# Linear attention into two mixture layers: the first batch's q loaded by tokens and turned on TensorE, its product in fp32, and two late weights in place of four

## The chip, the cores and the metric

The kernel runs on one core of a Trainium2 chip. The metric is the device time of one launch in microseconds (us), the median of three runs, lower is better. A core has five instruction queues that run beside each other: TensorE (PE in the rows, with PEld for its weight loads), VectorE (DVE), ScalarE (ACT), GpSimd (POOL) and SyncE (SP), which here issues nearly all DMA transfers. Each queue is worked off strictly in order, so an instruction that waits holds up all that stands behind it on its engine.

## The reference

q, k, v have shape (8 batches, 8 heads, 576 tokens, 64); all data are fp32.

```python
kv = np.einsum('bhsd,bhse->bhde', k, v)
out = np.einsum('bhsd,bhde->bhse', q, kv)
rms = np.sqrt(np.mean(out * out, axis=-1, keepdims=True) + 1e-06)
x = out / rms * g_norm                      # then 4608 tokens x 512
h = np.maximum(x @ w_in1, 0.0)              # 512 x 2048
x = (s * (h * h) + b) @ w_out1              # 2048 x 512
h = x @ w_in2
out = (h / (1.0 + np.exp(-h))) @ w_out2
```

## The kernel before, in words

The 4608 tokens are cut into nine blocks of 512 (`T`). Blocks 0 to 7 are the first 512 tokens of each batch; the ninth holds the 64 tokens (`REM`) that each batch has left over. Attention goes by pairs of heads, four pairs (`p`) in a batch, in `attention_pair`; `z` marks batch 0. A pair forms k'v on TensorE (`kv`, tile `kv_ps`), copies it out (`kv_out`, tile `kvf`, for batch 0 lent from a weight tile as `lent_wi10`), multiplies q by it (`o`, tile `o_ps`), does the same for the left-over tokens (`rem`, tile `r_ps`), and `normalize` squares (`sq`), sums (`part`, `ms` with tile `m_ps`), takes the root (`rms`), inverts (`inv`), spreads and scales to x. `split_x` then splits x into a rounded part `xh` and a rest `xl`.

A product of near-fp32 quality is made of three fast products on such halves (`mm3`: lines 208, 209, 210). So q of every pair is turned by VectorE (line 517, after four loads in which each run is 32 floats long), rounded on ScalarE (`q_hi`) and its rest taken on VectorE; k'v is split likewise (`kv_hi` and the `kvl` rest).

The first layer does blocks 0 to 4 directly. One unit (`unit`) is one of 16 slices of the hidden width: four products with `wi<m>` make tile `h` (12 matmuls), ScalarE and VectorE turn it into `gh`, four products with `wo<m>` add to the output sums `acc` (12 matmuls). The other blocks and the second layer use a scheme with seven products per four (lines 933 and 1074 to 1076). Before a weight can be used its 8-byte form must be loaded into `raw` and decoded by `decode`: ScalarE `mag`, VectorE `sign` and `top`, ScalarE `carry`, GpSimd `total`, ScalarE `hi`, VectorE `lo` (lines 309, 313, 318, 326, 332, 214, 220). Block 0 thus runs while the 32 weights of layer 1 are being decoded, in the order wi0, wi1, wo0, wi2, wo1 and so on.

Of these 32 the last `LATE` in that order are decoded otherwise: their room is taken from the decode buffers, so they are loaded, each in two halves (128x256), only after all the others are done and `turn` has closed the pool. With `LATE = 4` these are wo13, wi15, wo14 and wo15.

What order each queue gets is decided in Python at build time by `Plan.run`: it replays all steps with costs written beside them (`add(engines, key, ...)`) and issues, engine by engine, the step that it believes can start next, the smaller key first. While the replay's clock is under 40 it fills TensorE with small products on zeros (`warm_up`, line 1267, tile `warm`). These costs set the order alone; on the chip the queues wait for real events. Tiles in PSUM come from few banks: four under `acc`, two under `h`, two under `at`.

Of the kernel before, what the change touches and what calls it, by code (L numbers as in the profile page):

```python
# [133 lines left out]
def kernel(  # L134
# [36 lines left out]
    LATE = 4  # L171
# [111 lines left out]
    def decode(layer, kind, m, c, width, sfx, key, needs=(), quarter=None, made=()):  # L283
# [60 lines left out]
        add({"SP": 0.48}, key - 5 - 0.8 * (layer == 0 and (kind, m) == ("i", 1)), load, needs=needs, makes=[f(0)], takes=[raw], move=width * P * 8 / 3.6e5)  # L344
        key -= 0.5
# [101 lines left out]
    def attention_pair(bb, p, key, before=None):  # L447
# [11 lines left out]
        b["psk"], b["pso"], b["psr"] = ("at", ("k", me)), (acc, ("o", me)), ("at", ("r", me))  # L459

# [82 lines left out]
        for i in range(P // Q):  # L543
# [9 lines left out]
        add({ACT: 0.2}, key + 0.4, kv_hi, needs=[f("kvf")], makes=[f("kvh")], takes=[b["kvs"]], gives=[b["kvf"]])  # L553
        add({DVE: Port(0.2)}, key + 0.5, lambda e: rest(e, st["kvl"], st["kvf"], st["kvh"]), needs=[f("kvh")], makes=[f("kvl")],
            gives=[b["kvf"]])
        add(dve(S), key, q_turn, needs=[("q", bb, p, i) for i in range(P // Q)], makes=[f("qT")], takes=[b["qT"]],
            gives=[b["q"]])
        add(act(T), key + 0.4, q_hi, needs=[f("qT")], makes=[f("qh")], takes=[b["qs"]], gives=[b["qT"]])
        add(both(T), key + 0.5, lambda e: rest(e, st["ql"], st["qT"][:, :T], st["qh"]), needs=[f("qh")], makes=[f("ql")],
            gives=[b["qT"]])  # L560
        add({"PE": 0.682}, key + 1.5, o, needs=[f("kvl"), f("ql"), f("kvh"), f("qh")] + prev,
            makes=[f("o")], takes=[b["pso"]], gives=[b["kvs"], b["qs"]])
        add({"PE": 0.2}, key + 2.2, rem, needs=[f("kvf"), f("qT")], makes=[f("r")], takes=[b["psr"]],
# [5 lines left out]
        normalize(bb, p, key + 2, [f("o")], [b["pso"]], lambda: st["pso"])  # L569

    def normalize(t, p, key, needs, gives, src):
# [7 lines left out]
        def sq(e):  # L579
            st["sq"] = ap.tile([P, T], F32, tag="sq", name="sq")  # L580
# [28 lines left out]
        def x(e):  # L609
# [6 lines left out]
        add(act(T), key, sq, needs=needs, makes=[f("sq")], takes=[("sq", me)])  # L616
# [5 lines left out]
        add(dve(T), key + 0.8, x, needs=[f("spread")] + ([("x32", t, p - 1)] if p else []), makes=[("x32", t, p)],  # L622
            takes=[("x32", t)] if t < TP and p == 0 else [], gives=[("sq", me)] * (t < TP) + gives)
# [82 lines left out]
    def unit(u):  # L706
# [51 lines left out]
        add({ACT: 0.62} if layer == 0 else act(T), u + 0.3, g_hi, needs=[src], makes=[("gh", u)], takes=[gs])  # L758
# [384 lines left out]
    with tc.manual_schedule():  # L1143
# [10 lines left out]
        rem_t = ap.tile([P, 2, 2 * D], F32, name="rem_t")  # L1154
        lent["rem"] = lend("wo12")
        for t in (lent["rem"], rem_t):
            nc.gpsimd.memset(t[REM:], 0.0)
# [3 lines left out]
        for t in kvf_t:  # L1161
            nc.gpsimd.memset(t, 0.0)
# [161 lines left out]
```

## Time and profile before

| | before |
|---|---|
| median of three runs | 1564.57 us (1561.56 to 1564.99) |
| the profiled execution's own time | 1562.31 us |
| its span, first to last instruction | 1560.5 us |
| TensorE busy | 1539.7 us, 99% |
| VectorE busy | 1084.5 us, 69% |
| ScalarE busy | 854.7 us, 55% |
| GpSimd busy | 635.1 us, 41% |

A busy TensorE is not TensorE at work that counts: the products on zeros are busy time too, and an instruction's time in a row holds some 0.2 us of pipeline that overlaps the next one. The profiled execution is 2.26 us shorter than the median; 1.81 us of its time lie outside the span.

### The profile page before, as it was taken

The page shows a single profiled execution, that of the slowest core. Times are in us where ns is not written, and L with a number is a line of the kernel's source. Part 1 is how long each engine was busy: PE and PEld are TensorE (multiplying, and loading weights), DVE is VectorE, ACT ScalarE, POOL GpSimd, SP SyncE. Part 2 cuts the span into 40 slices and gives each one's busy share as a digit, 9 for nine tenths or more (in the row PEclk, how much of TensorE's full clock was granted, in tenths as well). Part 3 has the DMA queues.
Part 4 walks back from the last instruction along what each step waited for, and adds up shares of the span by engine and source line. Part 5 has one row for each costly group of instructions (what it writes and reads, how often), then busy time and mean ns, then how long its engine had stood idle before and what let it go on. Part 6 is the DMA issues. An engine that isn't in the chain of part 4 may idle for free.

```text
span 1560.5 us, 23102 instructions
## 1 busy us (share of the span) xinstructions
PE 1539.7 (99%) x7394; PEld 1259.0 (81%) x7394; DVE 1084.5 (69%) x1925; ACT 854.7 (55%) x1693; POOL 635.1 (41%) x584
## 2 busy tenths in 40 slices
PE   8998999999999999999999999999999999999998
PEld 6776878888888878888888788888888888888887
DVE  6887678878777577888888766775676566666521
ACT  5886566557666576667666544544454444444222
POOL 2331122111125234587548832772376246622410
PEclk9999999999999999999999999999999999999999
DMA  8855689988557878898988876878687766876684
GB/s 217 214 163 133 212 252 286 272 251 242 187 183 222 282 233 270 274 291 264 326 271 295 276 266 192 257 194 243 193 261 189 255 190 216 195 248 201 199 196 149
DMA packets 351514, 361.24 MB, mean 231 GB/s; under 512 B 175392, under 2 KB 236832, under 8 KB 351392
## 3 DMA queue, kind: packets, MB, share of 16 engines
q1 hardware_dynamic: 351264, 359.76, 76.4%
q8 instruction: 59, 0.97, 0.3%
q14 instruction: 63, 0.52, 0.1%
q0 software_dynamic: 128, 0.00, 0.0%
HBM read 272.63 MB, written 87.03 MB: 230 GB/s over the span
## 4 chain that ended last, share of the span: by engine, by line
PE 89%; DMA 4%; SPq 2%; DVE 2%; ACT 1%; issue 1%; POOL 0%; DVEq 0%; ACTq 0%
PE hp L933 28%; PE acc L1074 9%; PE acc L1075 9%; PE acc L1076 9%; PE h L208 5%; PE h L209 5%; PE h L210 5%; PE acc L208 4%; PE acc L209 4%; PE acc L210 4%; SPq L236 2%; DMA raw<-in_moe_w_out_dram 1%; PE kv_ps L503 1%; PE acc L773 1%; PE acc L772 1%; PE acc L774 1%
## 5 line engine op out<-in xcount | busy, mean ns | idle before, releaser
L933 PE MATMUL hp<-xo,win 128*128 128x512 f32 x2016 | 509.2, 390 | 1.1 <-DVE g L220 0.9
L933 PEld LDWEIGHTS hp<-xo,win 128*128 128x128 f32 x2016 | 377.1, 188 | 82.9 <-DVE tmp L958 4.1
L220 POOL TENSOR_TENSOR g<-tmp,g 128x512 fp32r<-128x512 f32 x192 | 249.3, 1307 | 306.2 <-ACT g L214 276.2
L1074 PE MATMUL acc<-g,wout 128*128 128x512 f32 x672 | 261.8, 390 | 0.8 <-DVE ya L1085 0.5
L1076 PE MATMUL acc<-g,wout 128*128 128x512 f32 x672 | 261.6, 389 | 0.0
L1075 PE MATMUL acc<-g,wout 128*128 128x512 f32 x672 | 261.5, 389 | 0.0
L1083 DVE TENSOR_TENSOR ya<-acc,ya 128x512 f32<-128x512 f32 x168 | 115.7, 689 | 128.3 <-PE acc L1076 120.6
L1074 PEld LDWEIGHTS acc<-g,wout 128*128 128x128 f32 x672 | 126.1, 188 | 28.0 <-DVE ya L1085 0.9
L1076 PEld LDWEIGHTS acc<-g,wout 128*128 128x128 f32 x672 | 126.1, 188 | 26.5
L1075 PEld LDWEIGHTS acc<-g,wout 128*128 128x128 f32 x672 | 126.2, 188 | 26.1
L214 ACT ACTIVATE g<-tmp 128x512 fp32r<-128x512 f32 x192 | 119.3, 629 | 24.4 <-PE acc L1076 10.3
L208 PE MATMUL acc<-gh,wo 128*128 128x512 f32 x320 | 131.2, 410 | 1.3 <-ACT wo L214 1.3
L739 ACT ACTIVATE h<-h 128x512 f32<-128x512 f32 x96 | 55.9, 582 | 139.0 <-PE h L210 137.0
L332 POOL TENSOR_TENSOR rq<-raw 128x256 uint32<-128x256 uint32 x72 | 47.2, 655 | 197.6 <-DVE raw L318 149.4
L208 PE MATMUL h<-xh,wi 128*128 128x512 f32 x320 | 126.9, 397 | 0.0
L1110 POOL TENSOR_TENSOR ya<-ya 128x512 f32<-128x512 f32 x84 | 108.1, 1316 | 45.7 <-DVE ya L1083 35.7
L209 PE MATMUL acc<-gh,wo 128*128 128x512 f32 x320 | 125.6, 392 | 0.6 <-DVE gh L222 0.4
L210 PE MATMUL acc<-gh,wo 128*128 128x512 f32 x320 | 125.4, 392 | 0.3 <-DVE wo L220 0.2
L209 PE MATMUL h<-xl,wi 128*128 128x512 f32 x320 | 125.4, 392 | 0.0
L210 PE MATMUL h<-xh,wi 128*128 128x512 f32 x320 | 125.2, 391 | 0.0
L958 DVE TENSOR_TENSOR tmp<-hp,tmp 128x512 f32<-128x512 f32 x144 | 98.9, 687 | 23.8 <-PE hp L933 19.5
L993 ACT ACTIVATE hp<-hp 128x512 f32<-128x512 f32 x96 | 55.6, 582 | 95.6 <-DVE hp L973 95.3
(164 smaller groups left out, 2685.1 us busy)
## 6 DMA issues: line engine op xcount, KB each, us to landing
wout<-wo SPq DMA_DIRECT2D x368, 256.0 KB, 4.1
win<-wi SPq DMA_DIRECT2D x144, 512.0 KB, 5.0
wi<-rq SPq DMA_DIRECT2D x96, 256.0 KB, 3.1
wo<-rq SPq DMA_DIRECT2D x96, 256.0 KB, 3.5
win<-wi SPq DMA_DIRECT2D x80, 256.0 KB, 4.1
raw<-in_moe_w_out_dram SPq DMA_DIRECT2D x38, 256.0 KB, 4.1
raw<-in_moe_w_in_dram SPq DMA_DIRECT2D x34, 256.0 KB, 4.2
q<-in_q_dram SPq DMA_DIRECT2D x112, 72.0 KB, 3.0
```

Of the source, the lines that this page charges most:

```text
L208: nc.tensor.matmul(ps, wh, xh, start=first, stop=False)
L209: nc.tensor.matmul(ps, wh, xl, start=False, stop=False)
L210: nc.tensor.matmul(ps, wl, xh, start=False, stop=last)
L214: nc.scalar.activation(hi, src, AF.Copy)
L220: eng[e].tensor_tensor(lo, src, f32(hi), op=ALU.subtract)
L933: nc.tensor.matmul(to, w[:, wn, f_], x_[:, xn], start=first and n == 0, stop=kk == KH - 1 and n == 2, skip_group_check=True)
L958: nc.vector.tensor_tensor(t, bank[me, a], tmp[b_, me], op=ALU.add)
L1074: nc.tensor.matmul(to, w[:, 0, dd], gh, start=a == 0, stop=False)
L1075: nc.tensor.matmul(to, w[:, 0, dd], gl, start=False, stop=False)
L1076: nc.tensor.matmul(to, w[:, 1, dd], gh, start=False, stop=a == 1)
L1083: nc.vector.tensor_tensor(y2[tp, i, d], st["ps"], y2[tp, i, d], op=ALU.add)
L1110: eng[e].tensor_tensor(y2[tp, i, d], y2[tp, i, d], y2[tp, j, d], op=ALU.add)
```

## The change

Four parts, all of the start of the kernel but the last. One: for batch 0, q is loaded as k and v are, with tokens on the 128 partitions, in one transfer a pair (`load_q0`), with one more for the left-over tokens of all heads (`load_q0_rem`); TensorE turns it by eight products with the identity (`q0_turn`, tile `q_ps`), ScalarE copies it out into token order (`q0_out`), and the product with k'v is one fp32 product (`o`) on `kvf` itself, without the halves. The left-over tokens are turned by TensorE later (`q0_rem_turn`, behind unit 1's products). Two: the squares of batch 0 go into the lent q tile in place of the one tile `sq`, and x gives that tile free. Three: the small loads of s, b and g_norm go to the front of GpSimd's queue, and the work on them becomes steps of the plan (`signs`, `norm_weights`, `offsets`). Four: `LATE = 2`, so wo13 and wi15 are decoded with the rest and only wo14 and wo15 are late. Some keys move with it.

```diff
-    LATE = 4
+    LATE = 2
...
+        def load_q0(e):
+            st["q"] = lend_flat(wtag["q"], 2 * T // P * D)
+            dma(
+                st["q"].rearrange("p (h c d) -> p h c d", h=2, d=D), q[bb, hh, :T, :].rearrange("h (p c) d -> p h c d", p=P)
+            )
+
+        def load_q0_rem(e):
+            lent["qrem"] = lend_flat("wo13", H * D)[:REM]
+            dma(lent["qrem"].rearrange("p (h d) -> p h d", d=D), q[bb, :, T:, :].rearrange("h p d -> p h d"))
+
+        def q0_turn(e):
+            lent["z", p] = lend_flat(wtag["qT"], 2 * DM)
+            st["psq"] = psum(b["psq"], "q_ps")
+            t = st["q"].rearrange("p (h c d) -> p h c d", h=2, d=D)
+            for c in range(NCH):
+                for j in range(2):
+                    nc.tensor.matmul(st["psq"][j * D:(j + 1) * D, c * P:(c + 1) * P], t[:, j, c, :], ident, start=True, stop=True)
+
+        def q0_rem_turn(e):
+            st["psr"] = psum(b["psr"], "r_ps")
+            nc.tensor.transpose(st["psr"][:, :REM], lent["qrem"][:, p * P:(p + 1) * P], ident[:REM, :REM])
+
+        def q0_rem_out(e):
+            st["qT"] = lent["z", p][:, T:T + REM]
+            copy(e, st["qT"], st["psr"][:, :REM])
...
+        def q0_out(e):
+            copy(e, lent["z", p][:, :T].rearrange("p (t c) -> p t c", t=P), st["psq"].rearrange("p (c t) -> p t c", t=P))
...
+            if z:
+                nc.tensor.matmul(st["pso"], st["kvf"], lent["z", p][:, :T], start=True, stop=True)
+            else:
+                mm3(st["pso"], st["kvh"], st["kvl"], st["qh"], st["ql"], True, True)
...
+        if z:
+            add({"SP": 0.48}, lk, load_q0, makes=[f("q")], takes=[b["q"]], move=0.73)
+            if p == 0:
+                add({"SP": 0.63}, lk + 5.9, load_q0_rem, makes=[("qr0",)], takes=[("wo13", 0)], move=0.4)
+        for i in range(0 if z else P // Q):
...
+        if z:
+            add({"PE": 0.5}, key + 0.2, q0_turn, needs=[f("q")], makes=[f("qt")], takes=[b["psq"], b["qT"]], gives=[b["q"]])
+            add({ACT: 0.56}, key + 0.25, q0_out, needs=[f("qt")], makes=[f("q32")], gives=[b["psq"]])
+            add({"PE": 0.95}, key + 1.5, o, needs=[f("kvf"), f("q32")], makes=[f("o")], takes=[b["pso"]])
+            add({"PE": 0.2}, key + 2.1, q0_rem_turn, needs=[("qr0",), f("kvf"), ("mm1o", 1, KD - 1)], makes=[f("qrt")], takes=[b["psr"]], gives=[("wo13", 0)])
+            add({ACT: 0.15, DVE: 0.15}, key + 2.15, q0_rem_out, needs=[f("qrt")], makes=[f("qT")])
...
-            st["sq"] = ap.tile([P, T], F32, tag="sq", name="sq")
+            st["sq"] = lent["z", p][:, :T] if z else ap.tile([P, T], F32, tag="sq", name="sq")
...
-        nc.scalar.activation(gn, eps, AF.Sqrt)
+        nc.scalar.activation(guess, eps, AF.Sqrt)
+        lent["rem"] = lend("wo12")
+        nc.vector.memset(lent["rem"][REM:], 0.0)
+        nc.gpsimd.dma_start(out=s_t, in_=s.rearrange("(o n) -> o n", o=1).to_broadcast([P, 1]))
+        nc.gpsimd.dma_start(out=b_t, in_=b.rearrange("(o n) -> o n", o=1).to_broadcast([P, 1]))
+        for j in range(2):
+            nc.gpsimd.dma_start(out=g0[j * D:(j + 1) * D, :], in_=g_norm.rearrange("(d o) -> d o", o=1))
...
+        add({DVE: 0.45}, -8, signs, needs=[("q32", 0, 0)], makes=[("signs",)])
+        add({ACT: 0.2}, -8, lambda e: nc.scalar.activation(root, mag_s, AF.Sqrt), needs=[("signs",)], makes=[("root",)])
+        add({DVE: 0.65}, -8, norm_weights, needs=[("root",)], makes=[("gn",)])
+        add({DVE: 0.3}, -1, offsets, needs=[("signs",), ("x32", 0, 1)], makes=[("b1",)])
...
-            split_x(0, p, -5 + 2 * p)
-        seq = [(t, p, KF * (t - 1) + (0.5 + (3.2 if t < LB else 1.6) * p if t > 1 else 0.75 + 3.4 * p)) for t in range(1, TP) for p in range(NP)]
+            split_x(0, p, -5.5 + 1.5 * p)
+        seq = [(t, p, KF * (t - 1) + (0.5 + (3.2 if t < LB else 2.0) * p if t > 1 else 0.75 + 3.4 * p)) for t in range(1, TP) for p in range(NP)]
...
-        last_block(KF * (TP - 2) + 9.5)
+        last_block(KF * (TP - 2) + 9)
```

The lists below give the instructions of one queue as they stand in the program; the number behind a name is that of its buffer.

SyncE's queue at the start of the program, before (`lent_wo<n>` are weight tiles that hold k, v and q of batch 0 meanwhile, `orem_d` is where left-over results go):

```order
L236 DMA lent_wo8_154<-in_k_dram 128x2x256
L236 DMA lent_wo8_154<-in_v_dram 128x2x256
L236 DMA lent_wo12_124<-in_k_dram 64x8x64
L236 DMA lent_wo12_124<-in_v_dram 64x8x64
L236 DMA lent_wo4_166<-in_q_dram 32x18x32 x4
...
L236 DMA lent_wo11_267<-in_v_dram 128x2x256
L236 DMA lent_wo7_292<-in_q_dram 32x18x32 x4
L236 DMA orem_d_76<-orem_241 128x64
L236 DMA raw_334<-in_moe_w_in_dram 128x4x256
L236 DMA raw_338<-in_moe_w_in_dram 128x4x256
```

and now, from the first q on:

```order
L236 DMA lent_wo4_155<-in_q_dram 128x2x256
L236 DMA lent_wo9_159<-in_k_dram 128x2x256
L236 DMA lent_wo9_159<-in_v_dram 128x2x256
L236 DMA lent_wo5_166<-in_q_dram 128x2x256
...
L236 DMA lent_wo13_193<-in_q_dram 64x8x64
L236 DMA lent_wo11_205<-in_k_dram 128x2x256
L236 DMA lent_wo11_205<-in_v_dram 128x2x256
L236 DMA lent_wo7_217<-in_q_dram 128x2x256
L236 DMA raw_235<-in_moe_w_in_dram 128x4x256
L236 DMA raw_240<-in_moe_w_in_dram 128x4x256
```

The sixteen q loads have become four, the store to `orem_d` no longer stands ahead of the first two weights (`raw`), and one load of left-over q is new.

ScalarE's queue around the decoding of the first weight wi0, before (`raw_334` is wi0, `raw_338` wi1):

```order
L581 ACTIVATE sq_358<-o_ps_326 128x512
L214 ACTIVATE xh_367<-x32_343 128x512
L231 COPY orem_387<-r_ps_290 128x64
L597 ACTIVATE rms_399<-m_ps_394,vecs_114 128x16
L214 ACTIVATE qTh_403<-lent_wi14_390 128x512
L309 ACTIVATE dw_422<-raw_334 128x512
L326 ACTIVATE raw_334<-raw_334 128x512
L231 COPY lent_wi10_129<-kv_ps_409 64x64 x2
L214 ACTIVATE kvh_444<-lent_wi10_129 128x128
L309 ACTIVATE dw_449<-raw_338 128x512
L581 ACTIVATE sq_458<-o_ps_376 128x512
```

and now, from the same step (`raw_235` is wi0, `raw_240` wi1, `lent_wi14` the turned q of head pair 3):

```order
L309 ACTIVATE dw_353<-raw_235 128x512
L231 COPY lent_wi14_338<-q_ps_339 128x512
L644 ACTIVATE rms_368<-m_ps_355,vecs_114 128x16
L326 ACTIVATE raw_235<-raw_235 128x512
L309 ACTIVATE dw_376<-raw_240 128x512
L326 ACTIVATE raw_240<-raw_240 128x512
L214 ACTIVATE xh_388<-x32_325 128x512
L628 ACTIVATE lent_wi14_338<-o_ps_372 128x512
L214 ACTIVATE xh_423<-x32_325 128x512
L214 ACTIVATE wi0_433<-dw_353 128x512
```

The roundings of k'v and q are gone; the copy of the turned q of pair 3 stands behind the first step on wi0, and the squares of pair 3 behind four steps on weights and one rounding of x.

TensorE's queue at the end of block 0, before (products with wi14, wo13 and wi15, between them attention of later batches):

```order
L208 MATMUL h_1549<-xh_630,wi14_1514 128x512
L208 MATMUL o_ps_1580<-qTh_1460,kvh_1544 128x512
...
L503 MATMUL kv_ps_1602<-rem_t_123 64x64 x2
L530 MATMUL r_ps_1632<-qT_1592,kvf0_127 128x64
L208 MATMUL acc_747<-gh_1553,wo13_1613 128x512
...
L208 MATMUL acc_919<-gh_1553,wo13_1613 128x512
L593 MATMUL m_ps_1689<-part_1645,pairs_of_133 128x16
L503 MATMUL kv_ps_1698<-kv_1630 64x64 x8
...
L208 MATMUL h_1714<-xh_367,wi15_1677 128x512
```

and now (h on `wi0` and `wi1` with the new x names is block 1):

```order
L208 MATMUL acc_562<-gh_1457,wo13_1475 128x512
...
L208 MATMUL h_1546<-xh_348,wi15_1513 128x512
...
L208 MATMUL h_1546<-xh_479,wi15_1513 128x512
L208 MATMUL h_1586<-xh_1559,wi0_433 128x512
...
L532 MATMUL kv_ps_1610<-kv_1518 64x64 x8
L208 MATMUL o_ps_1624<-qTh_1467,kvh_1532 128x512
...
L208 MATMUL h_1586<-xh_1600,wi0_433 128x512
L566 MATMUL r_ps_1652<-qT_1552,kvf0_129 128x64
L208 MATMUL h_1657<-xh_1559,wi1_496 128x512
...
L208 MATMUL acc_562<-gh_1522,wo14_1631 128x512
```

wi15 stands behind wo13 without a gap, and ahead of the first product with a late weight, wo14, there are now products of block 1.

## Rows read from the trace of the kernel before

**Rows 1.** The page: the span, and busy time, share and instructions by engine.

```profile
span 1560.5 us, 23102 instructions
...
PE 1539.7 (99%) x7394; PEld 1259.0 (81%) x7394; DVE 1084.5 (69%) x1925; ACT 854.7 (55%) x1693; POOL 635.1 (41%) x584
```

**Rows 2.** Windows, columns as the first row says, PEclk the granted clock.

```profile
core 0: us, PE busy (x) PEld busy (x) DVE busy (x) ACT busy (x) POOL busy (x), PEclk, DMA share, GB/s
50.00:80.00 30.00, 29.37 (x144) 23.04 (x143) 24.18 (x41) 24.93 (x48) 10.14 (x9) 1.00 0.76 194
...
129.50:142.50 13.00, 6.50 (x59) 4.82 (x57) 8.77 (x23) 7.01 (x20) 2.00 (x4) 0.82 0.69 161
142.50:145.00 2.50, 2.50 (x8) 2.02 (x7) 1.03 (x3) 1.04 (x3) 0.61 (x1) 0.55 0.69 183
...
200.00:300.00 100.00, 99.82 (x579) 80.27 (x580) 83.35 (x176) 60.95 (x145) 21.37 (x27) 1.00 0.91 270
```

**Rows 3.** Timeline of PE, 17 to 52 us: start, length, line, out<-in, count.

```profile
17.72 0.80 PE L503 MATMUL kv_ps<-lent_wo 128*64 128x64 f32 x20
...
30.60 0.48 PE L208 MATMUL h<-xh,wi 128*128 128x512 f32 x1
...
33.47 0.69 PE L503 MATMUL kv_ps<-kv 128*64 128x64 f32 x16
...
38.06 2.24 PE L1267 MATMUL warm<-zeros 128*128 128x256 bf16 x19
...
42.37 0.39 PE L210 MATMUL h<-xh,wi 128*128 128x512 f32 x1
42.60 0.39 PE L208 MATMUL o_ps<-qTh,kvh 128*128 128x512 f32 x1
...
45.89 0.47 PE L208 MATMUL acc<-gh,wo 128*128 128x512 f32 x1
...
51.08 0.39 PE L208 MATMUL acc<-gh,wo 128*128 128x512 f32 x1
```

**Rows 4.** Windows of 1 us in the loading stage.

```profile
9.00:10.00 1.00, 0.06 (x1) 0.00 (x0) 0.65 (x4) 0.81 (x4) 0.00 (x0) 1.00 1.18 301
10.00:11.00 1.00, 0.00 (x0) 0.00 (x0) 0.91 (x5) 0.00 (x0) 0.00 (x0) 1.00 1.09 161
...
13.00:14.00 1.00, 1.00 (x21) 0.88 (x18) 0.78 (x1) 0.00 (x0) 0.00 (x0) 0.50 1.17 261
...
20.00:21.00 1.00, 1.00 (x13) 0.90 (x10) 0.92 (x3) 0.98 (x3) 0.00 (x0) 1.00 0.27 51
```

**Rows 5.** Timelines of PE, DVE and ACT: instructions that a landing released.

```profile
6.88 0.34 PE L503 MATMUL kv_ps<-lent_wo 128*64 128x64 f32 x4 [0.93 <-DMA lent_wo<-in_v_dram]
...
13.17 0.78 DVE L517 STREAM_TRANSPOSE lent_wi<-lent_wo 128x576 f32<-128x576 f32 x1 [0.39 <-DMA lent_wo<-in_q_dram]
...
24.01 0.68 ACT L309 ACTIVATE dw<-raw 128x512 f32<-128x512 f32 x1 [0.44 <-DMA raw<-in_moe_w_in_dram]
...
31.25 0.68 ACT L309 ACTIVATE dw<-raw 128x512 f32<-128x512 f32 x1 [1.74 <-DMA raw<-in_moe_w_out_dram]
```

**Rows 6.** Timelines of DVE and PE at the hand-off to the late weights.

```profile
122.89 0.69 DVE L220 TENSOR_TENSOR wi<-dw,wi 128x512 fp32r<-128x512 f32 x1
...
134.67 0.50 PE L210 MATMUL acc<-gh,wo 128*128 128x512 f32 x1 [0.18 <-DVE wo L220]
...
140.29 0.61 PE L593 MATMUL m_ps<-part,pairs_of 128*128 128x16 f32 x2 [4.42 <-DMA raw<-in_moe_w_out_dram]
141.26 1.12 PE L503 MATMUL kv_ps<-kv 128*64 128x64 f32 x16 [0.36 <-ACT rms L597]
```

**Rows 7.** Groups by line, 0 to 36 us: count, busy us, mean ns.

```profile
L517 DVE STREAM_TRANSPOSE lent_wi<-lent_wo 128x576 f32<-128x576 f32 x4 | 3.1, 765 | 0.4 <-DMA lent_wo<-in_q_dram 0.4
...
L220 DVE TENSOR_TENSOR qTl<-lent_wi,qTh 128x512 fp32r<-128x512 f32 x4 | 2.7, 676 | 0.1
...
L214 ACT ACTIVATE qTh<-lent_wi 128x512 fp32r<-128x512 f32 x4 | 2.5, 621 | 1.5 <-DVE lent_wi L517 1.5
```

More of the change, by code (lines that the diff above doesn't have):

```diff
@@ L343, in decode @@
         f = lambda i: ("dec", i) + me
-        add({"SP": 0.48}, key - 5 - 0.8 * (layer == 0 and (kind, m) == ("i", 1)), load, needs=needs, makes=[f(0)], takes=[raw], move=width * P * 8 / 3.6e5)
-        key -= 0.5
+        first = layer == 0 and (kind, m) == ("i", 0)
+        add({"SP": 0.48}, -5 if first else key - 5 - 0.8 * (layer == 0 and (kind, m) == ("i", 1)), load, needs=needs, makes=[f(0)], takes=[raw], move=width * P * 8 / 3.6e5)
+        key -= 0.5 if first else 0.5
         add(act(width), key - 0.5, mag, needs=[f(0)],
@@ L552, in attention_pair @@
             takes=[b["kvf"]], gives=[b["psk"]])
[L553 to L563, printed above, removed]
+        if z:
[4 more added lines that the diff above has]
+            add({ACT: 0.15, DVE: 0.15}, key + 2.15, q0_rem_out, needs=[f("qrt")], makes=[f("qT")])
+        else:
+            add({ACT: 0.2}, key + 0.4, kv_hi, needs=[f("kvf")], makes=[f("kvh")], takes=[b["kvs"]], gives=[b["kvf"]])
+            add({DVE: Port(0.2)}, key + 0.5, lambda e: rest(e, st["kvl"], st["kvf"], st["kvh"]), needs=[f("kvh")], makes=[f("kvl")],
+                gives=[b["kvf"]])
+            add(dve(S), key, q_turn, needs=[("q", bb, p, i) for i in range(P // Q)], makes=[f("qT")], takes=[b["qT"]],
+                gives=[b["q"]])
+            add(act(T), key + 0.4, q_hi, needs=[f("qT")], makes=[f("qh")], takes=[b["qs"]], gives=[b["qT"]])
+            add(both(T), key + 0.5, lambda e: rest(e, st["ql"], st["qT"][:, :T], st["qh"]), needs=[f("qh")], makes=[f("ql")],
+                gives=[b["qT"]])
+            add({"PE": 0.682}, key + 1.5, o, needs=[f("kvl"), f("ql"), f("kvh"), f("qh")] + prev,
+                makes=[f("o")], takes=[b["pso"]], gives=[b["kvs"], b["qs"]])
@@ L564, in attention_pair @@
+        add({"PE": 0.2}, key + 2.2, rem, needs=[f("kvf"), f("qT")], makes=[f("r")], takes=[] if z else [b["psr"]],
             gives=[b["kvf"], b["qT"]])
@@ L614, in x @@
             )
-        add(act(T), key, sq, needs=needs, makes=[f("sq")], takes=[("sq", me)])
+        add(act(T), key, sq, needs=needs, makes=[f("sq")], takes=[] if z else [("sq", me)])
         add(dve(T), key + 0.2, part, needs=[f("sq")], makes=[f("part")], takes=[("part", me)])
@@ L621, in normalize @@
         add(dve(T), key + 0.7, spread, needs=[f("inv")], makes=[f("spread")], gives=[("rms", me)])
-        add(dve(T), key + 0.8, x, needs=[f("spread")] + ([("x32", t, p - 1)] if p else []), makes=[("x32", t, p)],
-            takes=[("x32", t)] if t < TP and p == 0 else [], gives=[("sq", me)] * (t < TP) + gives)
+        add(dve(T), key + 0.8, x, needs=[f("spread"), ("gn",)] + ([("x32", t, p - 1)] if p else []), makes=[("x32", t, p)],
+            takes=[("x32", t)] if t < TP and p == 0 else [], gives=[("sq", me)] * (0 < t < TP) + gives)
         if t >= TP:
@@ L756, in g_lo @@
             rest(e, st["g"][1], h_t[u], st["g"][0], b1 if layer == 0 else None)
-        add({ACT: 0.62} if layer == 0 else act(T), u + 0.3, g_hi, needs=[src], makes=[("gh", u)], takes=[gs])
+        add({ACT: 0.62} if layer == 0 else act(T), u + 0.3, g_hi, needs=[src] + [("b1",)] * (layer == 0), makes=[("gh", u)], takes=[gs])
         add({DVE: 0.69}, u + 0.35, g_lo, needs=[("gh", u)], makes=[("gl", u)], gives=[("h", u)])
@@ L1160 @@
         nc.gpsimd.memset(lent["kvf"], 0.0)
-        for t in kvf_t:
+        rem_t = ap.tile([P, 2, 2 * D], F32, name="rem_t")
+        for t in (rem_t[REM:], *kvf_t):
             nc.gpsimd.memset(t, 0.0)
```

46 lines of the change are left out of this document (20 added, 26 removed).

## The prediction

> **What bounds the kernel now.** I read the page first. TensorE is busy for 99% of the span [rows 1], but busy time counts the products on zeros, so I went on to windows. From 200 us on it has no air left: 99.82 us of 100 [rows 2]. What can be won lies ahead of that, and TensorE passes it on to the end nearly whole. The timeline of TensorE shows two places. The first is the start: the first product of the first layer begins at 30.60, the first with wo0 at 45.89, the first with wo1 at 51.08, and between them zeros are multiplied, as the 19 at 38.06 [rows 3]. The second is the hand-off to the late weights: from 129.5 to 142.5 TensorE is busy for 6.5 us of 13, and the granted clock then is 0.55 of full in the 2.5 us that follow [rows 2]; the waits end on a weight's rest and on a weight's load [rows 6]. In between, at 50 to 80, it is busy for 29.4 of 30 [rows 2].
>
> What holds the start? Windows of 1 us show the transfers: where k and v move, 301 GB/s; where q moves in runs of 32 floats, 161 at the same share of DMA time; and 51 at 20 us, where a store stands in SyncE's queue ahead of the first weights [rows 4]. The timelines give landings, as a released instruction starts just behind: left-over v at 6.9, q of pair 1 at 13.2, wi0 at 24.0, wo0 at 31.2 [rows 5].
>
> **The loads.** Behind the left-over v now come ten transfers of 256 KB (q0, then k, v, q of three pairs) and 128 KB of left-over q: 2.75 MB. All but the small one have the runs of k and v, so at 301 GB/s they take 9.1 us and q of pair 3 is there at 16.0. wi0 has 512 KB, 1.7 us more: 17.7 in place of 24.0. The other bound is 161 GB/s, which gives 24 again: no gain. I take 301, since the shape is that of k.
>
> **From q to the first product.** Removed from pairs 0 to 3 are VectorE's four turns and rests, 3.1 and 2.7 us, and ScalarE's four roundings, 2.5 us, beside the small ones of k'v [rows 7]. Added is a copy of 128x512 a pair on ScalarE, by the rounding's row 0.62 each. The row of k'v prices the new products: 20 rows for ten products, two by two, in 0.80 with a tail of 0.2, so 0.06 a step of 64 columns [rows 3]. The turn (sixteen rows of 128 columns, two by two) is then 8 x 0.12 = 0.95; if columns cost nothing, 0.5. The fp32 product (two rows of 512 columns that fill the array) is 2 x 8 x 0.06 = 0.95; if a row went as fast as those of the first layer, which follow each other in 0.23 [rows 3], 0.46. I take 0.95 for both, since that row is fp32 too.
>
> That product speaks against the change: the three that it replaces take 3 x 0.23 = 0.69. [...]
>
> Pair 3 is the last: q at 16.0, turned by 17.0; but on ScalarE its copy stands behind wi0's first step, which waits for wi0 till 17.7 and takes 0.68 [rows 5]. So the copy ends at 19.0, the product at 20.0. In TensorE's new order 49 products on zeros and one short product follow before the first of the layer; a zero costs 2.24 / 19 = 0.12 with the tail, 0.11 without [rows 3], so they take 5.4 us: 25.4 at the soonest. wi0 needs 6.6 us from landing to first use before (24.0 to 30.6) [rows 3, 5], which gives 24.3; ScalarE's new queue has eight pieces of some 0.6 between wi0's first step and its rounding, two of which wait for x from VectorE. I take 26.5; the bounds are 25.4 and, with two more pieces of waiting, 28.
>
> Next in the order are 24 products, 21 zeros and two short turns up to the first with wo0: 5.5 + 2.3 + 0.3 = 8.1, so 34.6. wo0 lands some 7.2 after wi0 as before [rows 5], at 25; before, it took 14.6 from there to its first product [rows 3, 5], with attention of pairs 2 and 3 on both engines; that as upper bound gives 39.5. I take 35.7. To the first product with wo1 the order has 21 products, 14 zeros and five short ones, 4.8 + 1.5 + 0.7: 42.7. Before it was 51.1, but two k'v (0.6 each without tail), a three-product o (0.7) and two short ones (0.3) of batch 1 had been done too, 2.2 us. Four zeros follow later in the new order, 0.4. **Start: 51.1 - 42.7 - 2.2 - 0.4 = 5.8 us won; bounds 2 and 8.**
>
> **The hand-off.** Before, idle time is 13 - 6.5 = 6.5. [...] Together 7.6. The pool is closed when wi14's rest ends, 122.89 + 0.69 = 123.6; wo13's last half lets a product go at 134.67 [rows 6], 11.1 us later. Now the pool closes when wi15 is done, so at the latest when its first product can go. From there to the first product with wo14 the order has 36 fast products (12 with wi15, 18 of block 1, 3 with wo13, 3 of attention), k'v and a short one: 8.3 + 0.8 = 9.1. What remains of the wait is 11.1 - 9.1 = 2.0. Ahead of wo15, whose loads stand on SyncE behind k, v and q of a later batch, there are 33 products more, 7.5 us; before, the k'v ahead of wi15 started 6.6 us after wo13's last half let go (141.26 - 134.67) [rows 6]. **Hand-off: 7.6 - 2.0 = 5.6 won; bounds 0 and 7.6.**
>
> **Costed at nothing.** The squares' own room: VectorE and ScalarE need one tile less, and no row shows a wait on it. Four small loads stand ahead of the identity on GpSimd; q0 lands at about 7.7, and if that cover were gone each us late would move the first turn by one. The left-over q is turned behind unit 1, four short products, counted above. Two more weights are decoded within block 0: about 1.9 us of ScalarE each (three rows like the 0.62 and 0.68), hidden if decoding starts 6 us sooner, as above.
>
> **Sum.** 1562.3 (the profiled execution's own time; span 1560.5 and 1.8 outside) - 5.8 - 5.6 = 1550.9. The median lies 2.3 above that execution, so I predict **1553**.
>
> **Rivals.**
> - *The hand-off stays.* The wait moves from wo13 to wo14 or wo15, for SyncE is worked off in order and the late halves still stand behind loads of k, v and q. For it: the 4.42 us wait ended on a load [rows 6]. Against: 9 us of other products now stand between. Then only 5.8 is won: 1558.8.
> - *Weights bound block 0.* TensorE starts sooner and then waits for decoding, as ScalarE is busy 24.9 us of 30 at 50 to 80 and VectorE 24.2 [rows 2]. Then the start's gain is lost and 5.6 stays: 1559.
> - *The loads don't get faster*, because each transfer waits in SyncE's queue for the landing of the eighth before it. wi0 then lands at 20 to 21, 3 us later than I count: 1556.
> - *Both of the first two*: within 3 us of before.
> - *Slower: the clock stays low at the start.* Before, after an idle stretch (0.06 busy at 9 to 10, none at 10 to 11), the granted clock was 0.50 at 13 [rows 4]. The new order puts no zeros between the turns and products of pairs 1 to 3, which wait for landings. [...]
>
> **Chances.** My case 0.58, hand-off stays 0.14, weights 0.11, loads 0.08, both 0.04, clock 0.05. What a measurement can tell from no change is 0.2%, 3.1 us: faster than 1561.4 are the first four, 0.91; I give 0.89 for faster, 0.06 for the same, 0.05 for slower. With the bounds of start and hand-off my own case lies between 1547 and 1558; the range reaches from 1547 to 1560, which leaves out the last two cases and the ends.
>
> **What would show it.** q of pair 3 as one load at about 16, wi0 used from about 18; first product of the layer at 25.5 to 28, with wo0 at 34.6 to 39.5, with wo1 near 43; granted clock 1.00 from 7 to 40; before wo14 an idle stretch of 0 to 4 us and no fall of the clock behind it; from 200 us on the same steps. I am wrong if wi0 lands at 21 or later, if TensorE waits for `gh` or weights by more than 2 us in all at 50 to 110, or if a wait of 4 us and more stands before wo14 or wo15.

## The result, and the profile after

The changed kernel takes 1549.77 us (median of four runs, 1549.24 to 1550.58), beside 1564.74 for the kernel before on the same chip: ratio 0.9909, 95% interval [0.9892, 0.9927]. A second set of four runs, made later beside other kernels, gave 1547.98 us and 0.9899 [0.9883, 0.9915]. So 14 to 16 us are won; 1553 was predicted, with 1547 to 1560 as range. The profiled execution took 1549.24 us, 13.1 less than that of before.

The page of the changed kernel, against [rows 1]:

```profile
span 1547.5 us, 23039 instructions
...
PE 1536.7 (99%) x7402; PEld 1255.4 (81%) x7402; DVE 1084.1 (70%) x1908; ACT 855.9 (55%) x1683; POOL 634.4 (41%) x584
```

TensorE's busy time fell by 3 us only, while the span lost 13: the rest was idle time. Where it went, windows of the changed kernel show, with columns as in [rows 2]:

```profile
50.00:80.00 30.00, 29.38 (x165) 23.69 (x164) 26.67 (x50) 25.43 (x51) 8.45 (x9) 1.00 0.88 228
80.00:115.00 35.00, 35.00 (x170) 27.53 (x169) 29.57 (x52) 29.77 (x57) 12.31 (x11) 1.00 0.67 187
115.00:145.00 30.00, 29.81 (x181) 23.55 (x180) 23.76 (x50) 22.43 (x53) 6.68 (x8) 1.00 0.56 144
200.00:300.00 100.00, 99.80 (x598) 80.65 (x597) 81.97 (x172) 61.89 (x143) 22.67 (x29) 1.00 0.91 278
```

and the same two middle windows of the kernel before:

```profile
80.00:115.00 35.00, 33.01 (x159) 25.37 (x158) 27.61 (x49) 28.73 (x56) 13.42 (x12) 1.00 0.63 178
115.00:145.00 30.00, 23.50 (x146) 18.64 (x145) 20.21 (x46) 16.50 (x40) 6.14 (x8) 0.89 0.55 133
```

The hand-off is full now: 29.81 of 30 busy at full clock, against 23.50 at 0.89. Two more microseconds came back at 80 to 115, where the prediction had counted nothing. From 200 to 300 us TensorE is as full as before [rows 2].

TensorE's timeline at the start of the changed kernel, against [rows 3]: turn and fp32 product of pair 3, the zeros behind them, then the first products with wi0, wo0 and wo1.

```profile
18.33 1.09 PE L501 MATMUL q_ps<-ident,lent_wo 128*64 128x128 f32 x16
...
20.60 1.02 PE L559 MATMUL o_ps<-lent_wi,lent_wi 128*128 128x512 f32 x2
21.46 3.98 PE L1321 MATMUL warm<-zeros 128*128 128x256 bf16 x35
...
26.87 0.48 PE L208 MATMUL h<-xh,wi 128*128 128x512 f32 x1
...
35.20 0.48 PE L208 MATMUL acc<-gh,wo 128*128 128x512 f32 x1
...
43.26 0.39 PE L208 MATMUL acc<-gh,wo 128*128 128x512 f32 x1
```

ScalarE's timeline there, against [rows 5]: the first step on wi0, and the copy of pair 3 behind it.

```profile
18.93 0.68 ACT L309 ACTIVATE dw<-raw 128x512 f32<-128x512 f32 x1
19.50 0.58 ACT L231 COPY lent_wi<-q_ps 128x512 f32<-128x512 f32 x1
```

wi0 is used 5.1 us sooner than before, and the first products come 3.7 (wi0), 10.7 (wo0) and 7.8 us (wo1) sooner.

Not all of it reached the end. Timelines of GpSimd, VectorE and TensorE in the second layer of the changed kernel:

```profile
868.12 1.28 POOL L220 TENSOR_TENSOR g<-tmp,g 128x512 fp32r<-128x512 f32 x1 [0.94 <-ACT g L214]
```

```profile
868.50 1.19 DVE L413 TENSOR_TENSOR rq<-rq 128x256 f32<-128x256 f32 x1 [2.85 <-DMA wo<-rq]
```

```profile
874.63 0.97 PE L980 MATMUL hp<-xo,win 128*128 128x512 f32 x3 [1.60 <-DVE tmp L1005]
```

and TensorE at the same place of the kernel before:

```profile
888.57 0.96 PE L933 MATMUL hp<-xo,win 128*128 128x512 f32 x3 [0.20 <-DVE tmp L958]
```

The clock behind it in the changed kernel:

```profile
876.70:880.10 3.40, 3.40 (x9) 2.65 (x9) 1.00 (x2) 2.25 (x5) 3.40 (x4) 0.50 0.75 229
```

TensorE waits there for VectorE, 1.6 us where before it was 0.2, and in this execution 3.4 us at half clock follow: nine products where 15 would fit at 0.23 each, so 1.4 us. Together nearly 3 us are given back.

The sum over the two profiled executions: start 51.08 - 43.26 - 2.2 - 0.4 (work that stands later, as in the prediction) = 5.2; 80 to 115 us 2.0; hand-off 6.3 of idle time and 1.1 of half clock, 7.4; given back 2.8. That makes 11.8 of 13.1; the rest lies in gaps too small to name.

### The profile page after: what moved, and what is told of

Same layout as the page of the kernel before. It is cut to its first block, busy times and chain, and to the rows that moved or that the text cites. A ratio compares the mean times of both kernels' runs of the same rounds, so it can differ in the third digit from the quotient of the medians.

```text
span 1547.5 us, 23039 instructions
## 1 busy us (share of the span) xinstructions
PE 1536.7 (99%) x7402; PEld 1255.4 (81%) x7402; DVE 1084.1 (70%) x1908; ACT 855.9 (55%) x1683; POOL 634.4 (41%) x584
## 4 chain that ended last, share of the span: by engine, by line
PE 88%; DMA 4%; DVE 3%; ACT 2%; SPq 1%; issue 1%; POOL 1%; POOLq 0%; ACTq 0%; DVEq 0%
PE hp L980 28%; PE acc L1121 10%; PE acc L1123 10%; PE acc L1122 10%; PE h L208 5%; PE h L210 4%; PE h L209 4%; PE acc L208 4%; PE acc L209 4%; PE acc L210 4%; DMA raw<-in_moe_w_out_dram 1%; PE kv_ps L532 1%; PE acc L820 1%; PE acc L819 1%; PE acc L821 1%; SPq L236 1%
## 5 line engine op out<-in xcount | busy, mean ns | idle before, releaser
L332 POOL TENSOR_TENSOR rq<-raw 128x256 uint32<-128x256 uint32 x68 | 43.5, 640 | 189.5 <-DVE raw L318 101.1
L214 ACT ACTIVATE rq<-rq 128x256 fp32r<-128x256 f32 x192 | 77.5, 413 | 63.4 <-POOL rq L332 28.9
```

The costliest lines, as they stand in the source:

```text
L214: nc.scalar.activation(hi, src, AF.Copy)
```

## The experiments

Two theories were at stake: that the start and the hand-off are two gains of about equal size, and that the start's gain is one of transfers (the run length of q) with the other parts costing nothing. The rivals put all of it into one place, or into another part of the start. Each run has its median beside the kernel before in the same set (1562.77 us for the first four, 1563.82 for the next four, 1564.11 for the last four):

| kernel | median, us | ratio to before, 95% interval |
|---|---|---|
| e1_late4: start alone | 1554.92 | 0.9946 [0.9933, 0.9958] |
| e2_only_late: hand-off alone | 1553.45 | 0.9945 [0.9932, 0.9957] |
| e3_last_block | 1547.63 | 0.9910 [0.9895, 0.9925] |
| e4_short_runs | 1553.20 | 0.9940 [0.9927, 0.9952] |
| e5_after_again: the change | 1547.98 | 0.9899 [0.9883, 0.9915] |
| e6_no_zeros | 1548.87 | 0.9906 [0.9892, 0.9920] |
| e7_one_square | 1553.82 | 0.9941 [0.9926, 0.9957] |
| e8_halves | 1556.42 | 0.9956 [0.9944, 0.9968] |
| e9_square_alone | 1565.15 | 1.0011 [1.0000, 1.0021] |
| e10_fp32_alone | 1561.35 | 0.9979 [0.9969, 0.9989] |
| e11_loads_alone | 1560.26 | 0.9970 [0.9959, 0.9982] |
| e12_fewer_zeros | 1548.45 | 0.9901 [0.9887, 0.9916] |

### The two halves apart

**Start alone.** The change with four late weights:

```diff
-    LATE = 2
+    LATE = 4
...
-            lent["qrem"] = lend_flat("wo13", H * D)[:REM]
+            lent["qrem"] = lend_flat("wi9", H * D)[:REM]
...
```

> The change with LATE = 4 again, so the start alone (the left-over q is lent from wi9 in place of wo13, which is a late weight again). My theory, two separate gains: the start's 4 to 6 us stay, the wait at the hand-off comes back with 6 to 8 us between 115 and 145 us and a fall of the clock behind it; 1556 to 1559 us. Rival, all of it is the start and the hand-off was won by the earlier decoding: 1549 to 1552. Rival, the start's lead is eaten by the decoding in block 0 and only the hand-off counts: 1562 to 1565.

**Hand-off alone.** The kernel before with

```diff
-    LATE = 4
+    LATE = 2
```

> The kernel before with LATE = 2 and nothing else, so the hand-off alone. My theory: block 0 starts as before (first product of the layer at 30.6, first with wo1 at 51) and the wait before the late weights shrinks from 6.5 us to 0 to 2; 1555 to 1559 us. Rival, two more weights to decode without the earlier start make TensorE wait within block 0, 4 us and more at 80 to 130: 1561 to 1565. Both parts together should give about the sum, 13 to 15 us, if they don't depend on each other.

Windows of the start alone, then of the hand-off alone:

```profile
80.00:115.00 35.00, 35.00 (x170) 27.32 (x168) 27.93 (x49) 27.16 (x52) 12.30 (x11) 1.00 0.59 161
115.00:145.00 30.00, 25.40 (x159) 19.21 (x158) 24.30 (x56) 21.48 (x54) 6.90 (x9) 1.00 0.72 178
```

```profile
80.00:115.00 35.00, 32.74 (x153) 25.33 (x152) 28.15 (x50) 28.73 (x55) 12.14 (x11) 0.95 0.64 178
115.00:145.00 30.00, 30.00 (x167) 24.40 (x166) 24.43 (x46) 24.56 (x53) 9.04 (x9) 1.00 0.53 131
```

Both rivals that put all into one place fall: each half wins by itself, 8.4 and 8.6 us by its ratio, each 1 to 2 us below my range. (The profiled executions lie off their medians: that of the start alone took 1551.54, 3.4 under, that of the hand-off alone 1557.02, 3.6 over; the clock of 0.95 belongs to it.) With four late weights 4.6 us stay idle at 115 to 145, less than the 6 to 8 that I expected and without the fall of the clock; with two none. The 2 us at 80 to 115 belong to the start: with it the window is full, without it it isn't. The halves add up to 17.0, the whole to 14.2 and 15.8; with intervals of some 2 us on each side it is not settled whether anything is lost between them.

### The run length of q

Each load of q in four, in runs of 32 floats, all else as in the change. The edit thus does two things: it shortens the runs, and it makes sixteen transfers of four.

```diff
-            dma(
-                st["q"].rearrange("p (h c d) -> p h c d", h=2, d=D), q[bb, hh, :T, :].rearrange("h (p c) d -> p h c d", p=P)
-            )
+            for half in (slice(0, Q), slice(Q, D)):
+                for h in range(2):
+                    dma(
+                        st["q"].rearrange("p (h c d) -> p h c d", h=2, d=D)[:, h, :, half],
+                        q[bb, 2 * p + h, :T, half].rearrange("(p c) d -> p c d", p=P),
+                    )
```

> The change with q of batch 0 still loaded by tokens, but each pair in four transfers whose runs are 32 floats, as the loads of before had; every engine's order but SyncE's is unchanged. My theory, the run length is what made the loads fast: where q moves 160 to 200 GB/s in place of 300, q of pair 3 and wi0 land 2.5 to 4 us later, first product of the layer at 29 to 31 in place of 26.9, and TensorE passes it on: 1551.5 to 1553.5 us. Rival, the loads are hidden behind the 5.4 us of zeros and the decoding: first product within 0.7 us of 26.9, 1549 to 1550.3.

Windows of the change, then of this kernel, in the loading stage, and ScalarE's first step on wi0 in this kernel:

```profile
10.00:11.00 1.00, 1.00 (x24) 0.78 (x22) 0.69 (x4) 0.17 (x2) 0.00 (x0) 1.00 1.10 349
```

```profile
10.00:11.00 1.00, 1.00 (x23) 0.77 (x23) 0.59 (x4) 0.28 (x2) 0.00 (x0) 1.00 0.93 135
...
14.00:15.00 1.00, 0.78 (x20) 0.64 (x20) 0.00 (x0) 0.19 (x1) 0.00 (x0) 1.00 0.73 116
```

```profile
23.41 0.66 ACT L309 ACTIVATE dw<-raw 128x512 f32<-128x512 f32 x1 [1.52 <-DMA raw<-in_moe_w_in_dram]
```

The loads are slower: 135 and 116 GB/s against 349. wi0 is used 4.5 us later, the first product starts at 31.51 in place of 26.87 (28.76 in the second execution of the change), and by the ratios (0.9940 against 0.9904, the mean of the two of the change) 0.36%, 5.6 us, are lost. So the zeros don't hide it.

Whether the run length is the cause, this run doesn't show. SyncE's timelines, first q and wi0 with wi1, in the change and then in this kernel:

```profile
3.16 0.62 SPq L236 DMA_DIRECT2D lent_wo<-in_q_dram  x1
...
10.63 1.45 SPq L236 DMA_DIRECT2D raw<-in_moe_w_in_dram  x2
```

```profile
3.18 2.65 SPq L236 DMA_DIRECT2D lent_wo<-in_q_dram  x4
...
19.10 1.17 SPq L236 DMA_DIRECT2D raw<-in_moe_w_in_dram  x2
```

SyncE spends some 0.67 us on issuing each of the four small transfers (2.65 us), about as much as on one of 256 KB (0.62). Twelve more of them are an estimated 8.0 us of its queue, and wi0 is issued 8.5 us later. The DMA share of 0.73 at 14 to 15 us says that the transfers did not fill the DMA engines there. Short runs do cost something by themselves, as 135 GB/s at a share of 0.93 against 349 at 1.10 says. But shorter runs without more transfers were not run, so the loss belongs to both together.

### The other parts of the start, each undone

**No zeros ahead of the first product**, beside the change itself in the same set:

```diff
+            warm.append(None)
+            if 42 < len(warm) - 1 <= 91:
+                return
             nc.tensor.matmul(warm[0][:, :2 * P], zeros[:, :P], zeros, start=True, stop=True)
```

> The change itself once more, for the three kernels that run beside it: 1549 to 1552 us, 11 to 14 us below the kernel before.

> The change without the 49 products on zeros between the fp32 product of pair 3 and the first product of the first layer; every other instruction and its order stays. If the clock falls in the idle stretch that this leaves (21.5 to 26.8 us), as it fell behind idle stretches of the kernel before: granted clock 0.50 for 3.4 to 6.8 us from about 27, 1.5 to 4 us lost, 1551 to 1554 us. If the zeros only fill time: 1549 to 1550.5. If the zeros are what holds the first product, as my sum had it (25.4 at the soonest by their count): first product before 26, and a gain of 1 us and more where the clock holds.

Windows and timeline of the kernel without these zeros:

```profile
25.50:27.00 1.50, 0.54 (x2) 0.50 (x2) 1.50 (x4) 1.15 (x2) 0.52 (x1) 0.52 0.90 314
27.00:32.40 5.40, 5.38 (x15) 3.40 (x15) 5.30 (x11) 4.84 (x10) 1.04 (x2) 0.50 0.42 118
```

```profile
22.22 1.02 PE L559 MATMUL o_ps<-lent_wi,lent_wi 128*128 128x512 f32 x2
...
27.02 0.80 PE L208 MATMUL h<-xh,wi 128*128 128x512 f32 x1
```

The granted clock did fall, to 0.50 from an estimated 25.6 (0.52 is the mean of 25.5 to 27) to 32.4, as the first case had it. From the fp32 product of pair 3 to the first product it now takes 4.80 us, with the zeros 6.27: they did hold it, by 1.5, as the third case had it in kind. The two nearly cancel: 0.9 us slower by the medians, which the intervals don't tell from nothing.

**One tile for the squares:**

```diff
-            st["sq"] = lent["z", p][:, :T] if z else ap.tile([P, T], F32, tag="sq", name="sq")
+            st["sq"] = ap.tile([P, T], F32, tag="sq", name="sq")
...
-        add(act(T), key, sq, needs=needs, makes=[f("sq")], takes=[] if z else [("sq", me)])
+        add(act(T), key, sq, needs=needs, makes=[f("sq")], takes=[("sq", me)])
...
```

> The change with the squares of batch 0 in the one tile sq again, as before; the planner gives other orders. My prediction costed the own room at nothing: 1549 to 1551 us. Rival, with TensorE's products now 2 us apart the squares of a pair wait for x of the pair before, 4 to 5 us for a pair: x of pair 3 ready at 31 and later in place of 28.6, the first unit's last products 2 to 5 us later: 1551 to 1555.

ScalarE's squares of the second pair and VectorE's x of pair 3 in this kernel, then that x in the change:

```profile
17.56 0.60 ACT L628 ACTIVATE sq<-o_ps 128x512 f32<-128x512 f32 x1 [1.91 <-DVE x L659]
```

```profile
34.80 0.75 DVE L659 SCALAR_TENSOR_TENSOR x<-o_ps,vecs,sq 128x512 f32<-128x512 f32 x1
```

```profile
27.83 0.74 DVE L659 SCALAR_TENSOR_TENSOR x<-o_ps,vecs,lent_wi 128x512 f32<-128x512 f32 x1
```

The rival is right: the squares of the second pair wait for x of the pair before, x of pair 3 comes 7 us later than in the first execution of the change (5.1 than in the second, whose loads came late), and 5.8 us are lost against the change in the same set. The planner gave other orders too, so this is the price of the one tile with the orders that go with it.

**The product on halves:**

```diff
-            if z:
-                nc.tensor.matmul(st["pso"], st["kvf"], lent["z", p][:, :T], start=True, stop=True)
-            else:
-                mm3(st["pso"], st["kvh"], st["kvl"], st["qh"], st["ql"], True, True)
+            mm3(st["pso"], st["kvh"], st["kvl"], st["qh"], st["ql"], True, True)
...
+            add(act(T), key + 0.4, q_hi, needs=[f("q32")], makes=[f("qh")], takes=[b["qs"]])
+            add(both(T), key + 0.5, lambda e: rest(e, st["ql"], lent["z", p][:, :T], st["qh"]), needs=[f("qh")], makes=[f("ql")])
```

(and the two steps for k'v's halves, as for later batches; the planner gives other orders here too).

> The change with the product of q and k'v of batch 0 made of three fast products on halves again (k'v and q rounded on ScalarE, rests on VectorE), the rest as in the change. If the fp32 product pays by the 0.62 and 0.68 us that it takes off ScalarE and VectorE for each pair: x of pair 3 ready 1.3 to 4 us later, first product of the layer 0.5 to 3 us later, 1550.5 to 1553.5 us. If TensorE's own time decides (0.95 us for one fp32 product, 0.69 for three): same or up to 1 us faster, 1548.5 to 1550.

VectorE's x of pair 3 and ScalarE's first step on wi0 in this kernel:

```profile
32.63 0.74 DVE L662 SCALAR_TENSOR_TENSOR x<-o_ps,vecs,lent_wi 128x512 f32<-128x512 f32 x1
```

```profile
22.82 0.66 ACT L309 ACTIVATE dw<-raw 128x512 f32<-128x512 f32 x1
```

This was missed by both: 8.4 us lost against the change, more than twice what the upper bound of the first allowed (1553.5, 3.7 above the first median of the change). In the set's own execution of the change, whose loads came equally late, x of pair 3 stands at 29.72, that step at 20.82 and the first product at 28.76; here they are 2.9, 2.0 and 3.1 us later (the product at 31.85). A part of that can be the granted clock, which was at 0.50 from 7.8 to 14.6 us here and from 8.7 to 12.2 there. No wait stands at the step on wi0: ScalarE comes to it late, and six roundings of q and k'v have gone through its queue by then. VectorE adds to it. Its step on wi0 with two inputs (line 318), here and then in that execution of the change:

```profile
27.74 0.65 DVE L318 SCALAR_TENSOR_TENSOR raw<-dw,raw 128x512 uint32<-128x512 uint32 x1
```

```profile
24.15 0.67 DVE L318 SCALAR_TENSOR_TENSOR raw<-dw,raw 128x512 uint32<-128x512 uint32 x1
```

It comes 3.6 us later: between ScalarE's step and this one, a rest of k'v and one of q have gone through VectorE's queue. At 65.8 us TensorE waits 1.8 us for `gh` on ScalarE, and half clock (0.50) from 69.2 to 72.6 follows; the other execution waits 1.5 us on VectorE at 73 without such a fall. So TensorE's own price, on which the second case rested, does not decide; what the rows show is the load on ScalarE and VectorE. The 3.1 us at the first product, 0.3 more of waiting and an estimated 1.4 for the half clock make 4.8 of the 7.2 us between the two executions; for the rest no row is named.

### The parts, each alone

Squares, then the fp32 product, each added to the kernel before; and the change with `LATE = 4`, one tile for squares and halves (the three edits above together), which leaves the loads with their turn. Each of these kernels also gets orders of its own from `Plan.run`.

```diff
+            lent["z", p] = st["qT"]
...
+            st["sq"] = lent["z", p][:, :T] if z else ap.tile([P, T], F32, tag="sq", name="sq")
...
```

> The kernel before with one part of the change: the squares of batch 0 go into the lent tile of the turned q, as in the change. If the parts of the start are links of one chain, each needed and none enough, q still lands late and wi0 at 24, so nothing is won: within 2 us of before. If the own room is worth by itself what its undoing cost in the change (about 5.8 us): 4 to 7 us faster.

```diff
+            if z:
+                nc.tensor.matmul(st["pso"], st["kvf"], st["qT"][:, :T], start=True, stop=True)
...
```

> The kernel before with one part of the change: the product of q and k'v of batch 0 as one fp32 product on k'v and q as VectorE turned it, without roundings and rests. Links of one chain: wi0 lands at 24 as before and its first use stays within 1.5 us of 30.6; 0 to 3 us faster. If it is worth by itself what its undoing cost (about 8.4 us): 6 to 9 us faster.

> The change with three parts undone: LATE = 4, the product on halves, the squares in one tile. What stays is the load of q by tokens with its turn on TensorE (and the small loads in front on GpSimd). Links of one chain: wi0 lands by 19 as in the change, yet x and the first product come late; within 3 us of before. If the loads carry the start by themselves, as undoing their run length cost about 5 us: 4 to 6 us faster.

Alone, squares give -1.7 us by the ratio (with an interval that ends at none), the fp32 product 3.3, the loads 4.7: 6.3 in all, against 8.4 for the whole start. Undone one by one they cost 5.8, 8.4 and 5.6, 19.8 in all, more than twice the start. So the parts depend on each other, as links of one chain do: squares and product are worth little while q is late, and their lack eats the gain of the loads. For the loads the links theory was too strict: 4.7 lies in the rival's 4 to 6. Part three, the small loads in front on GpSimd, was neither undone nor added by itself; what it is worth is within the figure of the loads.

### What is given back at 870 us

```diff
-        last_block(KF * (TP - 2) + 9)
+        last_block(KF * (TP - 2) + 9.5)
```

> The change with the key of the last block at 9.5 again in place of 9. In the change TensorE waits at 873 to 876 us for 2.0 us on VectorE and then has half the clock for 3.4 us, which the kernel before has only as 0.6 us and without the fall. Theory one, the moved key made it: the wait shrinks to under 0.7 us, no fall of the clock at 870 to 880, 1545.5 to 1547.5 us. Theory two, it comes from how the landing of that factor meets the chain at another time, or from another part of the change: the wait stays, 1548.5 to 1550.5.

GpSimd, VectorE and TensorE in this kernel, at the place of the 1.6 us:

```profile
867.37 1.44 POOL L220 TENSOR_TENSOR g<-tmp,g 128x512 fp32r<-128x512 f32 x1 [0.94 <-ACT g L214]
```

```profile
867.23 0.43 DVE L413 TENSOR_TENSOR rq<-rq 128x256 f32<-128x256 f32 x1 [2.33 <-DMA wo<-rq]
```

```profile
872.61 0.96 PE L980 MATMUL hp<-xo,win 128*128 128x512 f32 x3 [0.35 <-DVE tmp L1005]
```

In this trace the stall is gone, and the median of 1547.63 lies just beyond the edge of theory one; but the key is not the cause: the hand-off alone and the fp32 product alone have the key at 9.5 and a wait of 1.6, the start alone and the run length have 9 and 0.2. What tells them apart in all 14 traces is which engine comes first. Where VectorE's sum of 128x256 starts 0.04 to 0.72 us after GpSimd's product of 1.28 us, it takes 0.84 to 1.53 us in place of 0.43, and TensorE then waits 1.6 (six traces, the change's two among them). Where it starts 0.14 to 0.90 us before, TensorE waits 0.2 to 0.35 (eight). In twelve of the fourteen VectorE starts on a landing, so some tenths of a microsecond in a transfer decide over 1.4 us. In those six the sum ends 0.28 to 0.29 us behind GpSimd's product (in the change at 869.69, behind 869.40), whether it started 0.04 or 0.72 us after it. Order and times are measured; what holds the sum so long no run shows.

Then both findings together, the last block's key at 9.5 and the zeros cut in two:

```diff
+            if 72 < len(warm) - 1 <= 91:
+                return
...
-        last_block(KF * (TP - 2) + 9)
+        last_block(KF * (TP - 2) + 9.5)
```

> The change with the last block's key at 9.5 and 19 of the 49 products on zeros ahead of the first product left out (the 14 right ahead of it and 5 before those), 30 stay. First product of the first layer 0.5 to 1.3 us earlier than in the change when counted from the start of the fp32 product of pair 3 (6.3 us there), granted clock 1.00 all the way, and no wait over 0.7 us at 865 to 880: 1545 to 1547.5 us, 0.988 to 0.9895 of before. If the clock falls in the gap: 1547.5 to 1550.

TensorE's timeline:

```profile
22.17 1.02 PE L559 MATMUL o_ps<-lent_wi,lent_wi 128*128 128x512 f32 x2
...
26.98 0.50 PE L208 MATMUL h<-xh,wi 128*128 128x512 f32 x1 [0.17 <-ACT wi L214]
```

4.81 us in place of 6.27, no fall of the clock behind it (an early one, from 8.4 to 11.8, there is), and 0.2 at 870. Yet its median, 1548.45, misses the 1545 to 1547.5 that I expected, and its ratio, 0.9901, is that of the change: what the trace shows as 1.5 and 1.4 us can't be told in times whose runs spread over 3 to 4 us. No version here is shown to beat the change.

## Why the prediction was right, and where its steps were off

- **Loads.** Right in kind: by SyncE's timeline and the time to landing, q of pair 3 landed at 16.6 and wi0 at 18.7 (16.0 and 17.7 forecast), and wi0 is used at 18.93. But the sum went by the bytes and their runs alone. It left out SyncE's time for issuing, which four transfers in place of sixteen save, and the run above does not tell the two apart. The bound of 24 was mis-stated too: 2.75 MB at 161 GB/s end there, and wi0's 0.5 MB would come on top. Pair 3's turn at 18.33 waited not for q but for x of pair 0, as its weight loads show, a wait that I had not seen, and the fp32 product ended at 21.5 in place of 20.0.

```profile
18.33 0.85 PEld L501 LDWEIGHTS q_ps<-ident,lent_wo 128*64 128x64 f32 x16 [0.21 <-DVE x L659]
```

  The rival on the loads had its mechanism right: from 8.3 to 13.7 us each issue of SyncE starts right behind the landing of the eighth transfer before it (8.33 behind 8.22, 10.63 behind 10.61). It cost little, as the loads moved 332 to 370 GB/s at 8 to 12 us all the same.

- **Prices on TensorE.** The fp32 product takes 0.86 (20.60 to 21.46) and the turn 0.89 (1.09 less the tail of 0.2), 0.95 forecast for each.
- **First products.** 26.87, 35.20 and 43.26 for 26.5, 35.7 and 42.7. Zeros of 5.4 us did set the first (21.46 to 26.87). The start comes to 5.2 for 5.8; as a kernel of its own it is worth 8.4, of which 2.0 stand at 80 to 115 us.
- **Costed at nothing: squares and roundings.** Here the reasoning failed, though the sum did not. "No row shows a wait on it" was true of the kernel before, and there the own room indeed wins nothing (e9). In the new order, with the products close together, it is what lets the start through: 5.8 us. Likewise I priced the removed roundings and rests by their rows and put nothing of them into the sum, while putting them back costs 8.4 us, on ScalarE and VectorE ahead of wi0's weights and beyond.
- **Hand-off.** 7.4 for 5.6 (8.6 as a kernel of its own): the remaining wait of 2.0 did not come. The 7.6 of before are 6.5 of idle time and 1.1 of half clock: at a granted clock of 0.50 (138.0 to 144.7 us, the mean of 142.5 to 145 being 0.55 [rows 2]) k'v takes 1.12 in place of 0.69 [rows 3, 6], and eight products fill 2.5 us [rows 2], where eleven fit at 0.23 each. VectorE's and TensorE's timelines in the changed kernel (rest of the last weight before the pool closes, rest of the last half of wo14, first product with wo14 by the count of products):

```profile
122.74 0.69 DVE L220 TENSOR_TENSOR wi<-dw,wi 128x512 fp32r<-128x512 f32 x1
...
133.20 0.42 DVE L220 TENSOR_TENSOR wo<-rq,wo 128x256 fp32r<-128x256 f32 x1
```

```profile
133.64 0.40 PE L208 MATMUL acc<-gh,wo 128*128 128x512 f32 x1
```

  The pool closes at 123.43, as before (123.6), though two more weights are decoded by then, which the earlier start hides. The last half is ready 10.2 us later (11.1 counted) and the first product comes after 10.2 (9.1 counted): the two just meet.
- **Block 0.** The rival that weights bound it was wrong in sign: the waits of 2.0 us at 80 to 115 vanished. That, and the 2.8 us given back at 870, stood in no step.
- **Sum.** 1550.9 was worked out for the profiled execution, which took 1549.24. On it I put 2.3 us, the distance of the median before; after the change that distance is 0.5. The two make the 3.2 us between 1553.0 and 1549.8. That 1550.9 came so close is in part luck: start -0.6, hand-off +1.8, block 0 +2.0 and 870 us -2.8 nearly cancel, and 1.3 us have no row.
- **The clock.** In the profiled execution it is full from 6.3 us on up to 876. In that of the second set it was 0.50 at 8.8 to 12.1, behind an early wait for left-over v of 2.05 us, and full again soon after: the turn of 16 rows takes 1.98 us at 8.91 and 1.09 at 14.21. So it did not stay low, as the slower case had it. The length of that wait does not settle it alone: with the start alone it was 1.96 us, and the clock stayed full.

## What to carry to other kernels

Price a part of a change not by the waits of the kernel before but by the order that the whole change makes: a buffer on which nothing waits today can be what the new order stands on. Undo the parts one by one and add them one by one; where the first sums to more than the whole and the second to less, they are links of one chain. And read the run length of each early load and the number of transfers it is cut into, since they stand in one queue that is worked off in order and each took its time to issue: here 0.62 us for the first q as one transfer, 2.65 us for the same q cut into four.

## What the runs showed of the hardware

- Two executions of one program can differ by a fall of the clock. Windows of the second profiled execution of the change, with TensorE at 0.50 where the first has 1.00:

```profile
6.00:8.00 2.00, 0.21 (x8) 0.07 (x4) 0.00 (x0) 0.00 (x0) 0.00 (x0) 1.00 0.80 183
8.80:12.10 3.30, 3.19 (x23) 2.52 (x24) 0.39 (x3) 0.99 (x4) 0.00 (x0) 0.50 1.09 350
```

Its first product with wi0 starts at 28.76 in place of 26.87, yet it ends sooner (1548.88 us against 1549.24), for at 876 us it keeps full clock behind the same wait of 1.6. Of the 1.9 us at the start some 0.5 are the later landing of left-over v (8.26 in place of 7.76). Falls like these, an estimated 1.4 us each, can be a part of the spread between runs.

- An operation of 0.43 us on VectorE took 1.53 us where it started 0.04 us behind one on GpSimd, and TensorE waited 1.4 us more (loads alone, 882.48 us).
- SyncE took some 0.67 us to issue a transfer of 64 KB and 0.62 us for the first q of 256 KB (run length and change, at 3.2 us).
